# Which zero fills of a decode backward pass are narrow: nine, or six at other places

## The chip, the cores and the metric

The kernel runs on one core of a Trainium2 chip. A core has a matrix engine (TensorE, PE in the profile, with its weight loads as PEld), a vector engine (VectorE, DVE), a scalar engine (ScalarE, ACT), GpSimd (POOL) and SyncE (SP). Sixteen DMA engines move data between the device memory (HBM) and the on-chip memory (SBUF). The metric is the device time of one execution in microseconds (us). Before the change it is 600.77 us, the median of 6 runs that lie between 600.32 and 601.69.

## The reference: what is computed

The reference takes one token through an attention block and a gated feed-forward block, both modulated by `silu(c) @ w_mod`, and returns the output together with the gradients of ten inputs:

```python
mod = (_silu(c) @ w_mod).reshape(c.shape[0], 6, 1, -1)
h = _layernorm(x) * (1 + ca) + sa
x = x + ga * _A_ref(h, A_k_cache, A_v_cache, A_wq, A_wo)   # the last 4096 of 65536 positions
h = _layernorm(x) * (1 + cb) + sb
x = x + gb * _B_ref(h, B_w_gate, B_w_up, B_w_down)         # sigmoid gate, 3584 wide
_out, _vjp = jax.vjp(_f, A_x, A_k_cache, A_v_cache, A_wq, A_wo, B_w_gate, B_w_up, B_w_down, c, w_mod)
```

The gradients of the two caches have the caches' full size, 4 heads x 65536 positions x 128 in bf16, but the attention looks only at the last 4096 positions. All of the rest, 61440 positions in each of 4 heads of 2 tensors, has to be written as zeros. That is 120 MB out of some 186 MB that the kernel writes.

## The kernel before

The zeros are cut into 120 regions (`zregions`), each 128 rows of 8 KB, 1 MB. The kernel doesn't write them in one go. It has a list of all fills, `zleft`, and a function `zero(n)` that takes the next n of the list and issues them on POOL's queue. Calls of `zero` stand all over the kernel, with counts from tables (`Z_Q`, `Z_N`, `Z_B`, `Z_FFN`, `Z_END` and others), so that fills take what the loads and the gradient stores leave of the transfers' time. An optional second argument ties a fill to a matrix product, so that it isn't issued too early. The source of all fills is one tile of zeros, `zeros`, with 2 KB of one-byte floats in each partition; the transfer widens them to four-byte zeros. A semaphore belongs to each transfer from POOL, and eight of them are used in turn.

A fill has one of two forms. A *wide* one (L169) writes all 128 rows of its region. A *narrow* one (L162 and L165) is made of a reset of the cursor[...], a small forerunner of 5 rows with two pieces of 256 B each (2.5 KB, L162), and the fill itself, which writes only rows 8 to 127 of its region, as 60 x 2 rows (960 KB, L165). The constant `SKIP = 4` gives the forerunner its 5 rows (`NS = SKIP + 1`). The first 8 rows of each narrow region stay over. They lie in the first regions of the first tensor, and are written by the forerunners and by two transfers more, early in the run (`zero_rest`, L361 and L364), whose sizes grow with the number of narrow fills.

Which fills are narrow is told by the tuple `NARROW`: it holds places in the list, counted from 0. The regions with the lowest numbers are the narrow ones, and the loop over `narrow` and `wide` (L134 to L138) puts them at the places that `NARROW` names.

The rest of the kernel, in order of time:

- to some 60 us: loads of the caches, `wq` and parts of `w_mod` on SP's queue; the query and the scores
- to some 155 us: the matrices `N` of the attention backward (L636) over the four heads, paced by fills after each step
- to some 300 us: products with `wo` (L691), with loads of further parts of `w_mod` on POOL's queue and a fill after most steps
- to some 475 us: the feed-forward block in 7 steps (L1016 to L1061). Each loads a part of `w_up` and `w_gate` on POOL's queue (`load_ug`, L864) and of `w_down` on SP's (`load_wd`, L851), computes the gates and the gradients, and stores three gradients (L868, L854), with two to five fills
- to the end: the gradients of `wo`, `w_mod`, `wq`, V and K, all stored on POOL's queue (L1130, L1125, L1173, L1177, L1166), with the last fills among them

POOL's queue is worked through in order. A transfer that waits for its data, or for its semaphore's last transfer to land, holds up all that are behind it.

Of the kernel before, what the change touches and what calls it, by code (L numbers as in the profile page):

```python
# [34 lines left out]
SCALE = DH ** -0.5  # L35
KIB = 512
SKIP = 4
NARROW = (6, 18, 31, 44, 57, 70, 83, 96, 108)


def spread(total, n):
# [17 lines left out]
def kernel(  # L59
# [70 lines left out]

    narrow = zregions[0:len(NARROW)]
    wide = zregions[len(NARROW):]
    zleft = []
    while narrow or wide:  # L134
        if narrow and (len(zleft) in NARROW or not wide):
            zleft.append((narrow.pop(0), True))
        else:
            zleft.append((wide.pop(0), False))  # L138
    nlen = len(NARROW)
    ncount = list(range(1, nlen + 1))  # L140
# [1193 lines left out]
```

## Time and profile before

| | |
|---|---|
| median of 6 runs | 600.77 us |
| profiled execution | 600.9 us, span 599.1 us |
| busy share of the span | PE 68%, PEld 46%, DVE 55%, ACT 48%, POOL 27% |
| moved | 246.64 MB, mean 412 GB/s |
| POOL's transfers (q0) | 216.55 MB, 94.5% of 16 engines' span |
| SP's transfers (q1) | 29.37 MB, 12.6% |
| instruction fetches (q8) | 36 packets, 0.59 MB, 0.4% |
| wide fills | 111, 1024 KB each, 15.3 us from issue to landing |
| narrow fills | 9, 960 KB each, 15.3 us |
| forerunners | 9, 2.5 KB each, 13.7 us |
| the two remainders | 540 KB and 13.5 KB |

The span is the time from the first to the last instruction. Shares over 100% of DMA are possible, since packets of one engine overlap. A digit in the page's slices is the busy share of one fortieth of the span in tenths. "Issue to landing" of a transfer holds its time in the queue behind others. Behind each transfer the trace keeps the moments at which the DMA engines reported their share done, sixteen for each, but not which engine reported.

### The profile page before, as it was taken

The page shows a single profiled execution, that of the slowest core. Times are in us where ns is not written, and L with a number is a line of the kernel's source. Part 1 is how long each engine was busy: PE and PEld are TensorE (multiplying, and loading weights), DVE is VectorE, ACT ScalarE, POOL GpSimd, SP SyncE. Part 2 cuts the span into 40 slices and gives each one's busy share as a digit, 9 for nine tenths or more (in the row PEclk, how much of TensorE's full clock was granted, in tenths as well). Part 3 has the DMA queues.
Part 4 walks back from the last instruction along what each step waited for, and adds up shares of the span by engine and source line. Part 5 has one row for each costly group of instructions (what it writes and reads, how often), then busy time and mean ns, then how long its engine had stood idle before and what let it go on. Part 6 is the DMA issues. An engine that isn't in the chain of part 4 may idle for free.

```text
span 599.1 us, 11048 instructions
## 1 busy us (share of the span) xinstructions
PE 409.2 (68%) x4587; PEld 276.2 (46%) x4612; DVE 326.6 (55%) x620; ACT 284.9 (48%) x429; POOL 164.1 (27%) x265
## 2 busy tenths in 40 slices
PE   3997789999999989899974435534445196856300
PEld 3995434334344446556554334433434175655200
DVE  3654499999511020160008495794787887778430
ACT  3489515558201024212225665864867866863200
POOL 0003223213223222222232244333343252222230
PEclk9999699999999999999985555555555586755555
DMA  8999999999999999999999999999999999999996
GB/s 348 419 418 420 413 425 420 427 426 424 426 424 426 421 427 424 425 421 424 418 404 409 418 400 412 407 412 413 380 408 412 423 417 414 419 425 427 423 416 252
DMA packets 45171, 246.64 MB, mean 412 GB/s; under 512 B 5253, under 2 KB 5253, under 8 KB 24712
## 3 DMA queue, kind: packets, MB, share of 16 engines
q0 software_dynamic: 38976, 216.55, 94.5%
q1 hardware_dynamic: 6096, 29.37, 12.6%
q8 instruction: 36, 0.59, 0.4%
q14 instruction: 15, 0.12, 0.1%
q10 hardware_dynamic: 48, 0.01, 0.0%
HBM read 60.30 MB, written 185.60 MB: 410 GB/s over the span
## 4 chain that ended last, share of the span: by engine, by line
PE 34%; DMA 30%; DVE 19%; ACT 9%; issue 4%; POOL 0%; ACTq 0%; POOLq 0%; SPq 0%; DVEq 0%
DMA out_dram<-arena 14%; PE b_ps L691 13%; DMA out_dram<-zeros 7%; PE n_ps L636 6%; DMA arena<-in_B_w_down_dram 5%; DVE arena L210 4%; DVE junk L210 4%; ACT arena L241 4%; DVE arena L193 4%; DVE arena L206 3%; DMA arena<-in_B_w_gate_dram 3%; PE t_ps L598 2%; PE tp_wq L453 2%; PE w_ps L394 2%; ACT arena L837 1%
## 5 line engine op out<-in xcount | busy, mean ns | idle before, releaser
L169 POOL DMA_DIRECT2D out_dram<-zeros x111 | 60.5, 545 | 196.2 <-PE q_ps L471 50.1
L691 PE MATMUL b_ps<-arena 128*128 128x512 bf16 x494 | 113.4, 379 | 1.0 <-issue 0.2
L836 PE MATMUL tp_side<-ident_bf,arena 128*128 128x128 bf16 x432 | 52.4, 302 | 46.6 <-ACT arena L837 39.7
L837 ACT COPY arena<-tp_side 128x1024 bf16<-128x1024 bf16 x54 | 54.0, 1012 | 50.3 <-PE tp_side L836 49.8
L193 DVE TENSOR_TENSOR arena<-arena 128x2048 bf16<-128x2048 bf16 x64 | 76.5, 1223 | 2.3 <-PE n_ps L636 0.3
L691 PEld LDWEIGHTS <-arena 128*128 128x128 bf16 x512 | 48.8, 98 | 55.8 <-issue 2.9
L210 DVE CUSTOM_DVE_ANT_0 arena<-arena,scr 128x1024 bf16<-128x1024 bf16 x56 | 65.2, 1218 | 10.3 <-ACT scr L990 10.3
L636 PE MATMUL n_ps<-arena 128*128 128x512 bf16 x249 | 65.1, 378 | 6.9 <-DVE arena L193 5.0
L836 PEld LDWEIGHTS <-arena 128*128 128x128 bf16 x432 | 43.7, 140 | 51.2 <-issue 50.9
L241 ACT ACTIVATE arena<-scr,h 128x1024 bf16<-128x1024 bf16 x56 | 61.6, 1147 | 1.4 <-DVE dh2acc L210 1.3
L636 PEld LDWEIGHTS <-arena 128*128 128x128 bf16 x256 | 24.6, 97 | 41.6 <-issue 16.2
L1161 ACT ACTIVATE arena<-ps_kv 128x512 bf16<-128x512 f32 x48 | 26.1, 681 | 28.6 <-PE ps_kv L1157 28.3
L210 DVE CUSTOM_DVE_ANT_0 junk<-arena,b1k 128x1024 bf16<-128x1024 bf16 x28 | 34.2, 1222 | 9.9 <-DMA arena<-in_B_w_down_dram 9.4
L868 POOL DMA_DIRECT2D out_dram<-arena x28 | 21.1, 757 | 65.1 <-ACT arena L241 44.7
L202 DVE CAST arena<-b_ps 128x512 bf16<-128x512 f32 x6 | 4.2, 692 | 61.6 <-PE b_ps L691 61.6
L600 ACT CAST arena<-t_ps 128x512 bf16<-128x512 f32 x56 | 30.1, 589 | 12.1 <-PE t_ps L598 12.1
L1157 PE MATMUL ps_kv<-junk,arena 8*128 8x128 bf16 x256 | 27.2, 304 | 11.9 <-DVE arena L206 10.7
L1157 PEld LDWEIGHTS <-arena 8*128 8x128 bf16 x256 | 25.2, 140 | 13.7 <-issue 13.7
L455 ACT COPY arena<-tp_wq 128x1024 bf16<-128x1024 bf16 x23 | 21.7, 1041 | 8.0 <-PE tp_wq L453 8.0
L970 PE MATMUL fg<-hh_bf,arena 128*128 128x1 bf16 x224 | 8.2, 166 | 20.1 <-DMA arena<-in_B_w_down_dram 17.2
L877 ACT CAST arena<-fold_ps 128x512 bf16<-128x512 f32 x16 | 9.4, 587 | 24.1 <-PE fold_ps L875 24.1
L206 DVE TENSOR_SCALAR arena<-arena,cs_col 128x4096 bf16<-128x4096 bf16 (+1 forms) x16 | 16.1, 1022 | 8.4 <-DMA out_dram<-arena 8.4
(299 smaller groups left out, 642.4 us busy)
## 6 DMA issues: line engine op xcount, KB each, us to landing
out_dram<-zeros POOLq DMA_DIRECT2D x111, 1024.0 KB, 15.3
out_dram<-arena POOLq DMA_DIRECT2D x32, 1024.0 KB, 18.1
out_dram<-arena POOLq DMA_DIRECT2D x50, 512.0 KB, 9.7
out_dram<-zeros POOLq DMA_DIRECT2D x9, 960.0 KB, 15.3
arena<-in_A_wq_dram SPq DMA_DIRECT2D x8, 1024.0 KB, 20.4
arena<-in_A_wo_dram POOLq DMA_DIRECT2D x8, 1024.0 KB, 13.1
arena<-in_w_mod_dram POOLq DMA_DIRECT2D x7, 1024.0 KB, 19.0
arena<-in_B_w_down_dram SPq DMA_DIRECT2D x14, 512.0 KB, 8.7
```

The lines of the kernel that those rows point to most:

```text
L169: ins = nc.gpsimd.dma_start(out=region.bitcast(FP32), in_=zeros[:, :])
L193: return nc.vector.tensor_tensor(out=out, in0=a, in1=b, op=op)
L206: return nc.vector.tensor_scalar(out=out, in0=a, scalar1=s1, scalar2=None, op0=op0)
L210: return nc.vector.tensor_tensor_reduce(out=out, in0=w, in1=b, scale=1.0, scalar=0.0, op0=ALU.mult, op1=ALU.add, accum_out=acc)
L241: return nc.scalar.activation(out=out, in_=b, func=ACT.Copy, scale=col)
L600: nc.scalar.copy(out=o, in_=ps)
L636: mm = nc.tensor.matmul(nbank[k][:, :], lhsT=k_nat[:, g, t_ * DH:(t_ + 1) * DH], rhs=vp[:, t_ % 2, 4 * k:4 * k + 4, :].rearrange("p h d -> ...
L691: mm = nc.tensor.matmul(bbank[p][k][:, :], lhsT=a4[:, p, h, :], rhs=wo_t[u][:, a, k * 512:(k + 1) * 512], start=(i == 0 and a == 0), stop= ...
L836: nc.tensor.transpose(tp[:, i * P:(i + 1) * P], blk[:, i * P:(i + 1) * P], ident_bf[:, :])
L837: nc.scalar.copy(out=blk if dst is None else dst, in_=tp[:, :])
L1157: nc.tensor.matmul(ps[:, t4 * DH:(t4 + 1) * DH], lhsT=rows[32 * g:32 * g + HG, t_ * P:(t_ + 1) * P], rhs=hd[32 * g:32 * g + HG, :], start= ...
L1161: nc.scalar.activation(out=o, in_=ps[:, :], func=ACT.Copy, scale=float(scale))
```

## The change

The tuple of places gets six entries in place of nine:

```diff
-NARROW = (6, 18, 31, 44, 57, 70, 83, 96, 108)
+NARROW = (15, 45, 75, 95, 104, 113)
```

All else is derived from it. Six regions are narrow, so 114 fills are wide where 111 were. There are six resets and six forerunners. The two transfers of the remainder become smaller, 360 KB and 9 KB for 540 KB and 13.5 KB. The number of fills, the order of the list, the calls of `zero` and all bytes written stay as they were.

## The prediction

> **What bounds the kernel now.** I read four views in this order: the slices of the page, three long stretches with the busy time of each engine, the chain of work that ended last from 480 us on, and the fills as instructions on GpSimd (POOL). The slices show that the transfers never rest:
>
> ```profile
> DMA  8999999999999999999999999999999999999996
> GB/s 348 419 418 420 413 425 420 427 426 424 426 424 426 421 427 424 425 421 424 418 404 409 418 400 412 407 412 413 380 408 412 423 417 414 419 425 427 423 416 252
> ```
>
> The stretches (us; busy us of PE, PEld, DVE, ACT, POOL; clock; DMA share; GB/s) divide the run in three:
>
> ```profile
> 60.00:313.00 253.00, 230.99 (x1668) 119.50 (x1693) 109.31 (x160) 82.18 (x166) 65.80 (x111) 0.98 1.13 422
> 313.00:486.00 173.00, 79.15 (x1227) 66.79 (x1227) 122.38 (x269) 117.27 (x130) 63.02 (x95) 0.51 1.08 409
> 486.00:599.00 113.00, 53.09 (x754) 46.97 (x753) 64.75 (x129) 46.76 (x80) 28.54 (x43) 0.57 0.98 399
> ```
>
> Until 313 us the transfers run at their full rate and fills make up most of them. From 313 to 486 (the FFN) they have some 3% of air. After 486 they are saturated again, by stores; the lower mean there holds the empty tail. The last chain confirms it (start us, us, what): the long steps are landings of stores.
>
> ```profile
> 482.19 6.80 DVE arena L206 x16
> ...
> 489.29 16.67 DMA out_dram<-arena
> ...
> 506.51 21.85 DMA out_dram<-arena
> ...
> 544.15 19.77 DMA out_dram<-arena
> ...
> 566.95 14.50 DMA out_dram<-arena
> ...
> 581.97 0.55 POOLq L1329
> ```
>
> So the end is when the slowest of the 16 DMA engines has done its share. How far apart they are stands in the trace: each transfer leaves sixteen completion marks, one per engine. I sorted the sixteen of each transfer and took them against the ninth (us; "n" is a narrow fill; the last column is when the transfer landed):
>
> ```
> issued    first    15th    16th   landed
>  67.1     -1.0     0.80    0.92     77.2
>  68.3 n   -2.6     0.32    0.49     79.8
> 279.4     -8.9     2.51    2.53    299.6
> 284.2 n  -12.3     2.43    2.46    303.8
> 311.9     -6.2     1.76    1.78    326.8
> 353.6     -2.4     1.20    1.95    364.0
> 437.5     -0.7     1.25    1.41    445.7
> 460.0 n   -2.1     1.19    1.33    468.6
> 479.9     -0.6     1.20    1.32    486.0
> 512.0     -1.7     1.48    2.19    533.7
> 552.0     -1.9     1.34    2.97    571.5
> 582.0     -1.9     2.13    2.94    596.2
> ```
>
> One engine runs ahead, by 2.1 to 2.8 us more at each narrow fill of the first 300 us, up to 12.3 us; by 440 us the lead is gone; and over the last 90 us one engine falls behind, to 2.94 us at the last landing, 0.81 us after the next one.
>
> [...] 16 marks, one of them early by about one fill. [...] in the fills one stream of 8 KB packets takes 349 to 380 ns where the others take 348, and with the stores from 535 to 556 us one stream takes 311 to 342 ns where the others take 309.
>
> **The skipped engine's balance.** Between the narrow fill landed at 79.8 us and that at 303.8 us lie six more skips. A wide fill moves the landing by 2.45 us, so they are worth 6 x 2.45 = 14.7 us, but the lead grew only from 2.6 to 12.3, by 9.7. So the engine loses 5.0 us in 224 us, 2.2%. The lead then goes from 12.3 to 6.2 us in 23 us, far faster. The fill issued at 299.9 us has its first mark after 4.1 us, little more than one fill: this engine has caught up with what has been issued and idles. I read it so that most of the skips so far are wasted there. At 486 us it stands with the front group (first mark -0.6). I take the engine that comes last at the end to be the same one: it is again a single one with slow packets, and its lag stops growing (2.98 at 559.0 us) when they do. It goes from -0.6 to +2.94 in 110 us, 3.2%.
>
> **The change part by part.** The fills as instructions, and the two that cover the rest of the narrow rows (duration ns, min/median/max):
>
> ```profile
> L169 POOL DMA_DIRECT2D out_dram<-zeros x111: 532/534/671, 48.9 to 509.1; - x111
> L162 POOL DMA_DIRECT2D out_dram<-zeros x9: 593/603/612, 67.7 to 459.4; - x9
> L165 POOL DMA_DIRECT2D out_dram<-zeros x9: 653/672/689, 68.3 to 460.0; - x9
> L361 POOL DMA_DIRECT2D out_dram<-zeros x1: 568/568/568, 54.1 to 54.1; - x1
> L364 POOL DMA_DIRECT2D out_dram<-zeros x1: 537/537/537, 54.7 to 54.7; - x1
> ```
>
> 1. *Three narrow fills become wide.* For the other 15 engines nothing changes: 64 KB each either way. The landings agree: from 113.0 to 115.4 us with a narrow fill and its forerunner, 2.4; 2.45 for a wide one. I take 0 (bounds -0.1 and +0.1).
> 2. *The remainder shrinks with the count.* L361 goes from 540 to 360 KB. Its landing came 1.4 us after the one before (64.3 to 65.7), so two thirds is 0.93: 0.45 us gained on every engine at 66 us, in the stage that the transfers bind. L364 moved it 0.2 us, mostly fixed: 0. I take -0.45 (bounds -0.45 and 0, if the FFN swallows it).
> 3. *POOL* issues 603 + 672 ns for a narrow fill and 534 for a wide one: 3 x 741 = 2.2 us less. Nothing: POOL is busy 27% and mostly waits. Fill 104 (issued at 431.3 us) has 4.1 us of idle POOL behind it, fill 113 (480.7) some 2 us before the store at 485.2, which waits for VectorE. Without these gaps each would cost 0.74.
> 4. *The skips move*, from fills 6, 18, 31, 44, 57, 70, 83, 96, 108 to 15, 45, 75, 95, 104, 113; by count in the trace of before these were issued at 96.6, 176.5, 261.3, 359.2, 431.3 and 480.7 us. First stage: at 303.8 us seven skips have landed before and three after, so the first mark's engine stands at -12.3 + 4 x 2.45 = -2.5, with the last at +2.46: no landing is later. Likewise just ahead of its skips: about +0.7 at 108, +0.5 at 190 and +0.1 at 275 us (its place in the trace, -1.8, -6.8 and -9.7, plus 2.45 for each of one, three and four skips missing), where the last mark is at 1.6 to 1.7. Cost 0.
> 5. *FFN*: from -2.5 it loses 2.2 to 3.2% of 67 us, 1.5 to 2.1, and perhaps 2 us for two instruction fetches whose 16 KB packets (297.6 and 303.8 us) seem to fall on it: about +1 to +1.6 at 371 us, beside a last mark at 1.2 to 1.95. So not last, narrowly. Then a skip, some 2 us lost, a skip at 440, 1.5 lost. Cost 0 (bounds 0 and +2).
> 6. *Last stage*: before, it entered at -0.6; the skip of fill 113 now lands at 488 us with a queue of 5 to 10 us behind it, so the 2.45 us aren't idled away: at the end +2.94 - 2.45 = +0.5. The last is then today's 15th mark, +2.13: -0.81 (bounds 0, and -1.65, the gap at 565 us).
>
> Sum: -0.45 - 0.81 = -1.26 us. The profiled execution took 600.9 (span 599.1, and 1.8 around it), so 599.6; against the median of 600.77 this is 599.5, 0.21% less. From no change the measurement of this kernel can tell about 0.2%, 1.2 us.
>
> **Rivals.**
> *Slower: the skipped engine comes last in the FFN.* There PE waits for the landing of whole loads:
>
> ```profile
> POOL out_dram L868 <- ACT arena L241: 44.7, 9, 6.5
> ...
> PEld L970 <- DMA arena<-in_B_w_down_dram: 20.7, 9, 5.2
> ...
> PE fg L970 <- DMA arena<-in_B_w_down_dram: 17.2, 8, 4.9
> ```
>
> If the fall of 6.1 us after 303.8 us is slowness, and not idling, the engine stands at -2.5 + 6.1 = +3.6 by 327 us, 1.8 us behind today's last, and up to 3.5 us by 364. Each such us delays the w_down load on the path, and the late skips don't give it back. It decides from about 2.5 us on: 2.5 to 3.5 us lost less 1.26 is 602.0 to 603.0. Against it: first marks 4.1 us after issue.
> *The end stays.* The last engine at the end is not the skipped one, or fill 113's skip is idled away: only the 0.45 remains, 600.3. For it: the trace doesn't number engines.
> *More at the end.* The 15th mark was at only 1.34 until 571.5 us and was pushed late by events that needn't recur: 1.65 + 0.45 = 2.1 us, 598.7.
>
> **How the numbers follow.** The sum as worked: 0.50, own range 599.0 to 600.1, three fifths of it under 599.57; slower 0.13; the end stays 0.22; more at the end 0.15. Faster 0.30 + 0.15 = 0.45; within 0.2% 0.20 + 0.22 = 0.42; slower 0.13. The range from 598.4 to 601.0 leaves out the slower case and a bit of the last.
>
> **What would show it.** The L361 transfer lands 0.9 us after its forerunner; the lead of the first mark stays under 5 us; the FFN's start (313.1 us) comes 0.3 to 0.5 us sooner; at the last landing the 16th mark is near +2 and close to the 15th. Wrong would be: longer PE waits for w_down between 340 and 370 us with a 16th mark that stands alone there, or one that stands alone by 0.8 us at the end as today.

## The result

The changed kernel takes 599.52 us, the median of 18 runs (599.2 to 600.52), beside 600.75 us of the kernel before in 36 runs (599.98 to 607.2). The ratio is 0.9978 with a 95% interval of 0.9968 to 0.9989: it is faster by 0.22%, and the medians differ by 1.2 us. The profiled execution took 599.5 us, with a span of 597.7 us for 599.1.

### The profile after

The slices of the page are as they were, 9 everywhere:

```profile
DMA  8999999999999999999999999999999999999996
GB/s 349 418 419 422 412 425 414 427 421 427 429 418 425 422 429 422 423 423 421 425 396 410 422 409 414 410 408 408 409 409 416 413 404 412 422 422 427 424 417 283
```

The same bytes (246.64 MB) end 1.4 us sooner. What is different in the slices is the last one, 283 GB/s for 252: the tail is fuller, because the engines finish closer together (the last mark of the last store is 1.79 us behind the ninth, for 2.94). The instructions on the tile of zeros show that the change is in (duration ns, min/median/max; first and last start in us):

```profile
L169 POOL DMA_DIRECT2D out_dram<-zeros x114: 532/534/797, 49.6 to 508.5; - x114
L162 POOL DMA_DIRECT2D out_dram<-zeros x6: 593/606/614, 97.4 to 480.7; - x6
L165 POOL DMA_DIRECT2D out_dram<-zeros x6: 658/680/689, 98.0 to 481.3; - x6
```

The chain that ended last, from 480 us on, has the same steps as before (start us, us, what):

```profile
482.73 6.41 DVE arena L206 x16
...
491.20 14.56 DMA out_dram<-arena
...
506.31 21.93 DMA out_dram<-arena
...
543.46 19.06 DMA out_dram<-arena
...
565.58 14.48 DMA out_dram<-arena
...
580.57 0.56 POOLq L1329
```

Its start is no sooner than before (482.73 us for 482.19). The gain lies behind it: the step that began at 544.15 us begins at 543.46 and is 0.7 us shorter, and the last issue comes at 580.57 us for 581.97.

The completion marks of the transfers say where. In this table, read from the trace as in the prediction (marks in us against the ninth of the sixteen), each row is the same transfer in both kernels:

```
                            before                        after
                    1st   15th   16th  landed     1st   15th   16th  landed
fill 13            -2.2   0.49   0.50    97.0    -1.5   0.63   0.64    96.5
fill 83           -12.3   2.43   2.46   303.8    -2.9   3.11   3.49   303.3
w_gate, FFN start -10.6   1.68   1.76   313.0    -2.1   1.89   2.06   313.3
fill 104           -1.3   1.34   1.47   440.6    -2.4   2.09   2.33   440.8
fill 112           -1.4   1.18   1.32   483.4    -0.7   1.93   2.05   483.3
4th store of L1125 -1.7   1.63   2.12   536.2    -1.4   1.68   1.82   535.6
8th store of L1125 -1.9   1.36   2.75   563.9    -1.4   1.77   1.79   562.5
last store, L1177  -2.0   2.13   2.94   596.2    -1.6   1.74   1.79   594.8
```

The engine that ran ahead by up to 12.3 us no longer does. Up to fill 112 the landings differ by 0.5 us at most, in both directions. The one mark that stood alone at the end, 1.4 us behind the next at 563.9 us, has gone, and the landings are 1.4 us sooner. So all of the gain appears after 483 us.

### The profile page after: what moved, and what is told of

Its sections match the earlier page's. It is cut to its first block, busy times and chain, and to the rows that moved or that the text cites. A ratio compares the mean times of both kernels' runs of the same rounds, so it can differ in the third digit from the quotient of the medians.

```text
span 597.7 us, 11043 instructions
## 1 busy us (share of the span) xinstructions
PE 409.3 (68%) x4587; PEld 275.0 (46%) x4612; DVE 326.6 (55%) x620; ACT 284.8 (48%) x429; POOL 166.5 (28%) x262
## 2 busy tenths in 40 slices
DMA packets 45027, 246.64 MB, mean 413 GB/s; under 512 B 5085, under 2 KB 5085, under 8 KB 24544
## 4 chain that ended last, share of the span: by engine, by line
PE 40%; DMA 33%; DVE 15%; ACT 5%; issue 4%; POOL 1%; ACTq 0%; POOLq 0%; SPq 0%; DVEq 0%
DMA out_dram<-arena 23%; PE b_ps L691 18%; PE n_ps L636 6%; DMA arena<-in_B_w_down_dram 6%; DVE arena L193 4%; DVE arena L206 4%; DVE junk L210 2%; PE t_ps L598 2%; DVE arena L210 2%; DMA arena<-in_B_w_gate_dram 2%; PE tp_wq L453 2%; PE w_ps L394 2%; PE fold_ps L875 2%; DMA arena<-in_w_mod_dram 1%; PE tp_k L434 1%
## 5 line engine op out<-in xcount | busy, mean ns | idle before, releaser
L169 POOL DMA_DIRECT2D out_dram<-zeros x114 | 62.5, 550 | 200.8 <-PE q_ps L471 50.7
L655 ACT ACTIVATE arena<-n_ps 128x512 bf16<-128x512 f32 x8 | 4.3, 594 | 33.1 <-PE n_ps L652 33.1
## 6 DMA issues: line engine op xcount, KB each, us to landing
arena<-in_A_wo_dram POOLq DMA_DIRECT2D x8, 1024.0 KB, 12.3
```

Source lines behind the costliest of these rows:

```text
L169: ins = nc.gpsimd.dma_start(out=region.bitcast(FP32), in_=zeros[:, :])
```

## The experiments

The theory: one DMA engine is slower than the rest and came last at the end; a skip of it just ahead of, or within, the saturated last stage is the whole gain. The rivals: that there are fewer narrow fills (a smaller remainder, fewer instructions); that the early ones are spread differently; that any engine would do. A "skip" is a narrow fill; the first, 15th and 16th mark are those of the sixteen completion marks of a transfer, sorted, against the ninth. That a skip leaves one engine out is read from the marks of before: at each of the seven narrow fills of the first 300 us the first mark's lead is 1.7 to 3.1 us larger than at the forerunner just ahead, the second's by 0.65 at most, and a wide fill takes 2.45 us. That each of the sixteen marks is one engine's is my reading. Each ratio is to runs of the kernel before made beside the experiment (medians of 600.69 us for E1 to E4 and 600.66 for F1 to F4).

### E1: nine narrow fills as before, the last alone moved

```diff
-NARROW = (6, 18, 31, 44, 57, 70, 83, 96, 108)
+NARROW = (6, 18, 31, 44, 57, 70, 83, 96, 113)
```

> The nine places of before with the last one alone moved, 108 to 113. Theory (the end is what counts: one engine comes last there, and a skip just ahead of the saturated last stage holds its lead): 0.8 to 1.4 us less than before, and at the last landing the 16th mark near +2 and within 0.3 us of the 15th. Rival (fewer narrow fills, by their smaller remainder or fewer instructions): no difference. Rival (skips of the first half that were idled away): no difference.

Measured: 599.45 us, ratio 0.9978 (0.9969 to 0.9987). This one place is worth as much as the whole change. The view of spans and clock:

```profile
core 0: 597.7 us, clock 0.768
```

The first mark still runs ahead by 11.9 us at fill 83, as before, and it does no harm. At the last store the 15th and 16th marks are at 1.54 and 1.91.

### E2: the six of after, the last alone moved back

```diff
-NARROW = (15, 45, 75, 95, 104, 113)
+NARROW = (15, 45, 75, 95, 104, 108)
```

> The six places of after with the last one alone moved back, 113 to 108. Theory (the end): no gain over before, within 0.5 us, and one mark alone at the end, some 3 us after the ninth. Rivals (count of narrow fills; spread of the early ones): the whole gain of 1.2 us stays.

Measured: 600.44 us, ratio 0.9998 (0.999 to 1.0006). The gain is gone.

```profile
core 0: 598.6 us, clock 0.774
```

One mark stands alone again, at 3.10, with the 15th at 1.54. The skip is issued at 458 us here and at 481.3 us in after. It has no worth at the earlier place: by the landing of fill 112 the first mark is only 1.2 us ahead of the ninth, among a group. In the trace of before, which has its last skip at the same place, one can see where the lead goes: the first mark is 2.3 us ahead at 478.4 us and 0.9 at 484.7, a loss of over 20%, and there it comes 3.3 us after the store's issue (479.2 us). I read it as an engine that has run out of queued work.

### E3: six of the old places

```diff
-NARROW = (6, 18, 31, 44, 57, 70, 83, 96, 108)
+NARROW = (6, 31, 57, 83, 96, 108)
```

> Six of the places of before (6, 31, 57, 83, 96, 108), so the smaller remainder without new places. Theory: within 0.4 us of before; the last mark is alone at the end by 0.8 us or more, and the landings between 66 and 95 us are 0.4 us sooner, which is lost again by 300 us as in the trace of after. Rival (count of narrow fills): 0.45 to 1.2 us less than before.

Measured: 600.44 us, ratio 1.0001 (0.9989 to 1.0012); at the last store the marks are at 1.13 and 2.83, alone by 1.7 us. The count of narrow fills with its smaller remainder gives nothing that the times can tell. The expectation on its landings held in part: fill 13 lands at 96.4 us for 97.0, as expected, and by the start of the FFN most of it is lost (312.8 for 313.0), but the trace still has the last landing 0.5 us sooner, as E2 has. The times neither confirm nor exclude such a remnant.

### E4: a forerunner of four rows

```diff
-SKIP = 4
+SKIP = 3
 NARROW = (15, 45, 75, 95, 104, 113)
```

> The places of after, but the forerunner has 4 rows in place of 5[...]. If the slow engine of the fills and of the end is the one that SKIP = 4 leaves out: it has no relief, falls 2 to 3% of 240 us, 5 to 7 us, behind by 300 us, and the feed-forward stage starts 3 to 5 us later; 2 to 6 us more than before. If any engine will do, or the slow one at the end is another: as after, 1.2 us less than before.

Measured: 610.23 us, ratio 1.016 (1.0145 to 1.0174), 9.5 us more than before and more than expected. So the slow engine is the one that `SKIP = 4` relieves, and `SKIP = 3` at the same places gives it nothing; that another engine is left out in its place is my reading, since the traces have no engine numbers. With no relief one mark alone is at 8.74 at fill 83 (the 15th at 2.35) and at 5.94 at the last store. The FFN starts 4.2 us later than before (last load at 317.2 us), and from there to fill 112 takes 174.0 us for 170.0 in after. In the stretch of 313 to 486 us (columns as in the prediction; E4 enters the FFN later) the transfers move less than the 410 GB/s of after:

```profile
313.00:486.00 173.00, 74.64 (x1128) 64.64 (x1129) 117.93 (x252) 114.16 (x127) 60.77 (x91) 0.50 1.07 396
```

and the longest single wait of PE for `w_down` (last column, us) has grown from 5.2 to 8.1:

```profile
PEld L970 <- DMA arena<-in_B_w_down_dram: 25.2, 10, 8.1
PE fg L970 <- DMA arena<-in_B_w_down_dram: 21.4, 9, 7.8
```

### F1: the late skip later still

```diff
-NARROW = (15, 45, 75, 95, 104, 113)
+NARROW = (15, 45, 75, 95, 104, 119)
```

> The six places of after with the last moved on from 113 to 119, the last fill of all, issued at 509 us in the middle of the saturated last stage. Theory (only the skipped engine's balance at the last landing counts, once its queue is never empty): the whole gain of after, 1.2 us less than before; one mark stands alone until some 525 us and no longer. Rival (the skip has to come ahead of the stage, for the lag works through the transfers that wait for a landing): half of the gain or less.

Measured: 599.40 us, ratio 0.9976 (0.9966 to 0.9985), the whole gain. A skip that is issued at 510.8 us and lands at 530.0 serves as well as one that lands at 488.4. In this stage what counts is the engine's balance at the last landing, not the order on the way. The sign named for it came only in part: a mark stands apart only from 519 to 525 us, by 0.8 us at most (1.15 with the 15th at 0.36), and after the skip no longer (1.12 and 1.10 at 530.0).

### F2: no skip in the FFN

```diff
-NARROW = (15, 45, 75, 95, 104, 113)
+NARROW = (15, 45, 75, 113)
```

> The places of after without 95 and 104, the two of the feed-forward stage. By the prediction's step for that stage the skipped engine is at +1 to +1.6 at 371 us and loses some 2 us more by 440: the 16th mark stands alone, 1 to 3 us behind the 15th, from 380 us on, and the time is 1 to 3 us over that of after. Rival (the transfers have 3% of air there, as much as the engine is slower, so that it keeps up without skips): as after, within 0.4 us.

Measured: 601.42 us, ratio 1.0006 (0.9994 to 1.0018), so 0.3% over after, 1.9 us in the medians, as expected in size. The path was not: at fill 104 (landed at 440.6 us) the marks are still at 2.08 and 2.31, as in after with 2.09 and 2.33; only from 457 us on does one stand clearly apart (2.66 with the 15th at 1.85 at 463.9 us), to 3.27 with the 15th at 1.98 at fill 112. I read it so that the air of the FFN (410 GB/s in after, for 421 from 60 to 313 us) lets the slow engine keep up without a skip to some 450 us and no further. The late skip then starts from a worse place, and at the end one mark is alone at 3.48.

### F3: two late skips

```diff
-NARROW = (15, 45, 75, 95, 104, 113)
+NARROW = (15, 45, 75, 95, 104, 113, 117)
```

> The places of after and 117 as a seventh. Theory (after 113 the end is set by several other engines at about +1.7): as after, within 0.4 us, with the 15th and 16th marks near +1.7. Rival (the skipped engine is still among the last at the end): 0.3 us or more less than after.

Measured: 599.89 us, ratio 0.9994 with an interval of 0.9975 to 1.0012, too wide to tell it from after or from before (one of the ten runs took 605.28). The trace speaks for the theory: marks of 1.50 and 1.62 at the last store, and a span of 597.6 us beside 597.7. One late skip is enough, and a second finds nothing to shorten; by the times alone this stays unproven.

### F4: one skip alone

```diff
-NARROW = (6, 18, 31, 44, 57, 70, 83, 96, 108)
+NARROW = (113,)
```

> Only 113 is narrow, so the first stage and the feed-forward stage have no skip. Theory: the skipped engine falls 5 us behind by 304 us, the feed-forward stage starts 2 to 4 us later, and the run is 4 to 9 us slower than before, less than with another engine left out by about 2.5. Rival (skips of the first half are all idled away and were never needed): as after.

Measured: 608.08 us, ratio 1.0115 (1.0101 to 1.013). The loss of 7.4 us lies in the range expected. The early skips are needed, though not seven of them, since after has three. At fill 83 the 16th mark is at 8.75, where 5 was expected, and just as in E4 (8.74): E4's narrow fills are worth nothing there. At the last store it is at 3.64, 2.3 less than in E4. The two kernels enter the last stage with one mark equally far behind (3.76 and 3.61 at fill 112), and from there to the last store F4 takes 112.0 us and E4 114.5. These 2.5 us are the worth of one skip of the slow engine in the last stage; a fill moves a landing by 2.45 us. The medians differ by 2.2 us.

### The six kernels side by side

Where the time goes by stage, landings in us, each from one profiled execution (in brackets the count of narrow fills):

```
                       before   after   E1 (9)  E2 (6)  E3 (6)  F1 (6)
fill 13                  97.0    96.5    96.9    96.4    96.4    96.2
w_gate, FFN start       313.0   313.3   313.2   312.9   312.8   312.9
fill 112                483.4   483.3   483.2   483.0   483.1   483.0
last store              596.2   594.8   594.8   595.7   595.7   594.8
fill 112 to last store  112.8   111.5   111.6   112.7   112.6   111.8
```

The last row divides the kernels. Those with a skip at 113 or later need 111.5 to 111.8 us for the last stage, those without 112.6 to 112.8: 1.1 us between the means of 111.6 and 112.7. Of those not shown, F3 needs 111.3, and F2, which enters the stage with one mark far behind, 112.1. The row of fill 13 divides them by the count of narrow fills instead, and that difference is all but closed at the start of the FFN.

## Why the prediction was right, and where it was not

The time was right, 599.5 for 599.52, and so was the main cause. But the sum was right by two errors that cancel: -0.45 - 0.81 was forecast, and in the trace of after it is about 0 and -1.3. That it came out so near is luck.

*Part 1, three fills become wide: 0.* Nothing speaks against it. The 64 KB for each engine are an estimate from the sizes, 960 KB over the 15 engines that a skip leaves and 1024 KB over 16. E1 with nine narrow fills and after with six take the same time, 599.45 and 599.52.

*Part 2, the remainder: -0.45. This step failed.* The transfer itself shortened as worked out: it landed 0.93 us after the transfer before it (64.58 to 65.51), where it was 1.4 us, and 0.93 was the forecast. What failed is that the gain reaches the FFN: the prediction took it as made "in the stage that the transfers bind". The chain in the last 12 us ahead of the FFN, after:

```profile
299.13 0.83 PE fold_ps L875 x12
299.96 0.05 issue
300.02 1.69 PE b_ps L691 x7
301.70 0.02 issue
301.72 7.31 DMA arena<-in_w_mod_dram
...
311.21 10.35 DMA arena<-in_B_w_gate_dram
```

Up to 301.7 us it is TensorE that sets the time, where before it was landings of fills from 258.8 us on. In E1, E2, E3 and F1 the chain comes through fills as in before, in F2 and F3 through TensorE, and in all of them the FFN's last load lands at 312.8 to 313.3 us. So the two run level. The busy time of PE from 150 to 300 us in the kernel before (us of the stretch, busy us, clock, DMA share, GB/s), which the prediction did not use, says so:

```profile
150.00:300.00 150.00, 142.65 (x1128) 1.00 1.13 424
```

PE is busy 95% of it. So a shorter queue of transfers can buy little there. The sign that I named for it came out the other way: the FFN's last load lands at 313.3 us for 313.0, and its first products start at 311.1 us for 310.7. There is a second possible reason: in this trace the last mark, unlike the ninth, did not keep the 0.45. At fill 80 the ninth is 0.4 us sooner (291.5 us for 292.0), and the 16th 0.3 us later (293.9 for 293.7). In E2, E3 and F1 the 16th is 0.2 to 0.4 us sooner there. The two reasons are not separated, and which of them took the 0.45 stays open.

*Part 3, POOL: 0.* Right in effect. The first store behind fill 113 is issued at 485.8 us for 485.2. It holds POOL for 3.6 us and the second follows only at 489.4 us for 486.1, but E2, which has no narrow fill there, shows the same (485.2 and 488.8), and E1 and after end alike: the queue of the transfers is long enough to hide it. POOL's 254 transfers in after land in the order of their issue (before, 257), and one that waits holds up the rest: L169 alone waits 26 times for the landing of an earlier fill, 45.5 us in total (before, 26 and 44.6). These two stores land at 498.3 and 500.7 us, 2.4 us apart as before (498.5 and 501.0). Why that one issue takes so long in after, E2, E3, F1 and F3, and not in E1 and F2, stays open.

*Part 4, the first stage: 0.* Right. The skipped engine isn't alone behind at any of the landings compared. F4 and E4 show the price if it were: fill 83, which lands at 303.8 us before, lands 3.1 and 4.4 us later. The engine's slowness was put too low for this stage, however: 2.2% was read from how fast its lead grew. In E4, with no skip of it, its mark goes from 2.57 at 172.3 us to 4.43 at 228.2, 3.3%, and 8.74 at the landing of 308.2.

*Part 5, the FFN: 0 with "not last, narrowly".* Right in after. PE's waits for `w_down` are as before in their longest (us in total, times, longest):

```profile
PEld L970 <- DMA arena<-in_B_w_down_dram: 23.7, 12, 5.2
PE fg L970 <- DMA arena<-in_B_w_down_dram: 20.5, 12, 4.9
```

They are 3.0 and 3.3 us longer in total (20.7 and 17.2 before), but the first is so in E1, E2, E3 and F1 too (23.4 to 23.8 us, 12 waits), and E2 takes the time of before; so the longer waits don't belong to the new places. F2 shows how narrow it was: without the two skips one mark is alone from some 457 us on, and 1.9 us are lost. The slower rival, which needed 2.5 us, was off: it put the engine at +3.6 by 327 us, and in after the last mark there is at 1.99, with the 15th at 1.82. So it was not slowness that consumed the lead of before, which leaves idling. E1 has the same lead and E2 doesn't, and both are level at fill 112 (483.2 and 483.0).

*Part 6, the last stage: -0.81.* The mechanism was right, as E1, E2 and F1 show, and the size was off: -1.3 by the trace of after, -1.1 by the means of the table. Against the ninth the last mark went from 2.94 to 1.79. The term that was mis-sized is the place of the next engine. I took it from the last landing before, +2.13, where events between 571 and 590 us had pushed the 15th mark late. They didn't recur: it is 1.13 to 1.90 at the last store in E1, E2, E3, F1 and after. That was the rival "more at the end", which I gave 0.15. It held in its reason, not in its sum, since it too counted on the 0.45. (Its gap of 1.65 stands in the trace at 574.0 us; at 565 us it is 1.4.)

One thing the step didn't foresee: the lead that the skip gives is not kept in sight. In after the first mark is 2.19 us ahead at fill 113 (488.4 us) and 0.87 at fill 116 (495.7), where 3.3% would have taken 0.2 us, and the fills 114 to 116 had all been issued by 484.1 us. Later this engine can't be told from the others. Where that lead goes stays open; that the skip counts is shown by the ends of the runs, and by F4 against E4, where the slow engine is alone and can be followed.

## What to carry to other kernels

In this kernel the DMA engines are full to the end, and it ends with the slowest of them: before, the last mark came 2.94 us after the ninth and 0.81 us after the next. A mean share of 0.98 in the last stretch, the same before and after, doesn't show that; the spread of the completion marks of one transfer does. As I read the runs, relief of the slow engine was worth something only while its queue held work. Issued at 458 us, with 25 us of the FFN still to come, it was lost (E2, 600.44 us, no gain); given inside the last saturated stage, it counted in full (F1, 599.40 us). And from 150 to 300 us, where the transfers are never idle (424 GB/s), TensorE is busy 95% of the time, and a saving of 0.45 us that was forecast did not show at the FFN's start (313.3 us for 313.0): look at the next bound before a saving is counted.

## What the runs showed that I had not expected

- One of the 16 DMA engines alone is slower than the others, by 3.3% over 56 us of E4, and it is the one that `SKIP = 4` relieves: with `SKIP = 3` at the six places of after the kernel takes 610.23 us, 1.6% more than before. E1 to E4 ran on one chip and F1 to F4 on another, and the same setting relieves it on both (599.45 us in E1, 599.40 in F1). Which of the sixteen it is was not shown: the traces have no engine numbers, only a single mark that trails (8.75 with the 15th at 2.69 at fill 83 of F4).
- The slowness shows in single packets: in after, too, one stream of 8 KB packets takes 311 to 347 ns between 536 and 555 us where the others take 309 (before, 311 to 346, and not 342 as the prediction has it). In the fills the others don't all take 348 ns: of POOL's 8784 packets of 8 KB from 100 to 300 us of before, 6978 take that and 1163 take 322. The slow stream of the stores ends at 556 us, where PE has little left to do: it is busy 11.0 us of the 20 us up to there and 3.6 us of the 42 us after. Whether the two are connected was not tried.
- An engine that leads the others by 12 us costs nothing: in E1 its mark is 11.9 us ahead at fill 83, and the kernel takes 599.45 us, beside 599.52 of after.
